# Laying the VectorE work of a gelu over three steps of a hand-written order instead of two

## The chip, the core and the metric

The kernel runs on one core of one Trainium2 chip. Its time is the device time of one execution in microseconds (us); the figure compared is the median of several runs. The engines are named as the profile names them: PE is TensorE's matmul, PEld its weight load, DVE is VectorE, ACT is ScalarE, POOL is GpSimd, SP is SyncE, whose queue issues most DMAs.

## The reference, cut to what matters

```python
x = A_x                                             # 1 x 2048 x 640
xn = layernorm(x)
qkv = xn @ wqkv                                     # 32 heads of 20
p = softmax(q @ k.T * 20 ** -0.5)                   # per head, 2048 x 2048
A = (p @ v) @ wo
y = layernorm(xn)
B = gelu(y @ w1 + b1) @ w2 + b2                     # 640 -> 1536 -> 640, tanh gelu
out = x + A + B
```

## The kernel before

**Stages.** A first stage normalises the tokens and forms q, k and v (to about 245 us of the span). The second stage is the attention of all heads, with the MLP's matmuls and all other small work woven into it by hand. A tail multiplies the attention's output by `wo` and adds everything up.

**The attention loop.** Heads go in pairs g = 0 to 15, queries in halves hf = 0 and 1 of 1024. The list `ORDER` runs pairs 0 to 11 with both halves, then half 0 of pairs 12 to 15, then half 1 of pairs 12 to 15. Each (g, hf) has eight groups: two blocks of 512 queries by four groups of four key blocks, 256 groups in all. One group writes four `scores` (two matmuls L600 each, into a PSUM buffer of three; ACT's exp L602 into a tile `p`), and for key blocks 0 and 1 of the four DVE forms the tile `low` (L614, in `rest`). At the group's end stands `pv` of the group before (L631), which needs that group's `p` and `low`.

**Two ticks a group.** Small work is written as Python generators, each `yield` of which ends a step. Twice a group (after the scores of key blocks 0 and 1, and after those of 2 and 3) the loop calls `tick()`, which takes one step of each generator in the list `sides`, then one of each in the list `patient`. A number behind `yield` is a cost in us of DVE work. It acts in one way: when the steps of `sides` in this tick, or of a generator begun since the last tick, have announced any cost, `patient` is passed over.

```python
t, taken[0] = taken[0], 0.0
for its in (sides, patient):
    if its is patient and t > 0:
        break
    for it in list(its):
        r = next(it, self_end)
        if r is self_end:
            its.remove(it)
        else:
            t += r or 0.0
```

The first tick of a group is followed by `low` of key block 0 and then by `other()`, which writes some matmuls of the MLP (`layer1` L823, `layer2` L855) or of the projection (L932); the second tick is followed by `low` of key block 1 and by `pv`. The 256 groups have ticks 1 to 512. After the last group, `more` writes three projection matmuls at a time (one step of the projection) and then a tick, so a tick there comes as often as three matmuls end.

**The gelu.** When the last matmul of a `layer1` pair has been written, `begin(gelu(...))` takes the gelu's first step on the spot and puts the rest in `sides`; 48 gelus are begun in all. Its first DVE operation, L758, reads the PSUM tile `pu`; that pool (`psM`) has one buffer, so PE's next MLP matmul waits for it. L759, L762 and L763 follow on DVE, ACT's tanh is L766, and L768 to L770 write `hT`.

**Finishing a block of heads.** When all pairs of a block are through (blocks end after pairs 3, 6, 9, 12, 14 and 16, for each half), `unload` appends a generator `finish` to `fins`, and if it is the only one there, starts `finishing()`, which takes the finishes one after another:

```python
if len(fins) == 1:
    (sides if hf == 1 and g + 1 >= TAIL else patient).append(finishing())
```

A finish loads the row sums (`lt`, L692) and the two partial outputs (`oa`, L714), inverts the sums on DVE (L719 to L726), stores them (`linv`, L728), loads them spread over rows (`rb`, L740), and for each half of 512 columns adds (L744), multiplies (L746), casts (L748), subtracts (L750) and stores `oscr` (L751). The `oa` and `rb` tiles have one buffer each. Between loads and first uses stand empty steps, four in most places. It ends with `ready[hf] += 1`. In the last finish, that of pairs 15 and 16 in half 1, `rb` comes from matmuls on PE (L735) and its DMAs go through ACT's queue; it waits 24 steps for `lt` and 17 for `rb`.

**The weights of `wo`.** `prep_late` runs in `sides` near the end of the attention. It splits `wo` on DVE (L560 to L572) in one step of cost 1.0 and then five times three steps of cost 0.6, 0.7 and 0.7: sixteen ticks in a row in which `patient` is passed over.

**The projection.** The output has eight pieces of 256 tokens, four of each half; each needs its part of `oscr` (`ot`, L887) and the MLP's sum (`acc`, L888), loaded by `load_piece`, and has four accumulations of 15 matmuls (L932), each ended by DVE's L893; L895 stores the result. Piece 0 is loaded by `ahead()` in `sides`, once `ready[0]` is 6 (all blocks of half 0). Pieces 4 to 7 need `ready[1]` at 6. After the attention the accumulations take PSUM buffers from the pool of the scores, of three.

Of the kernel before, what the change touches and what calls it, by code (L numbers as in the profile page):

```python
# [42 lines left out]
def mha_mlp_kernel(tc, x, wqkv, wo, w1, b1, w2, b2, out):  # L43
# [4 lines left out]
    with (  # L48
# [463 lines left out]
        with ExitStack() as scope:  # L512
# [241 lines left out]
            def gelu(ps, r2f, hT, f):  # L754
                u = m1.tile([P, 2, MC], F32, tag="u", name="u")
                w = m1.tile([P, 2, MC], F32, tag="w", name="w")
                scale_rows(r2f)
                nc.vector.tensor_mul(u, ps, r2f[:, None, :].to_broadcast([P, 2, MC]))  # L758
                nc.vector.tensor_add(u, u, b1t[:, f : f + 2, None].to_broadcast([P, 2, MC]))  # L759
                yield 1.2  # L760

                nc.vector.tensor_mul(w, u, u)  # L762
                nc.vector.scalar_tensor_tensor(w, w, 1.0 / 0.044715, u, ALU.add, ALU.mult)  # L763
                yield 1.2
                yield
                nc.scalar.activation(w, w, AF.Tanh, scale=0.7978845608028654 * 0.044715)  # L766
                yield
                nc.vector.scalar_tensor_tensor(u, w, 1.0, u, ALU.add, ALU.mult)  # L768
                nc.vector.tensor_scalar(hT[:, f : f + 2, 0, :], u, ch, None, ALU.mult)
                nc.vector.scalar_tensor_tensor(hT[:, f : f + 2, 1, :], u, ch, hT[:, f : f + 2, 0, :],  # L770
                                               ALU.mult, ALU.subtract)
                yield 1.7

            def scale_rows(r2f):

                if r2f in unscaled:
                    unscaled.remove(r2f)
                    nc.vector.tensor_scalar(r2f, r2f, f1, None, ALU.mult)
# [34 lines left out]
            def layer1(mc, f):  # L813
                xnt, r2f = xs[mc]
                if f == 0:
                    hTs[mc] = m0.tile([P, KF, 2, MC], F16, tag="hT", name="hT")
                ps = psM.tile([P, 2, MC], F32, tag="m", name="pu")
                for i in range(2):
                    n = 0
                    fo_ = (f + i) % 4 * P  # L820
                    for k in range(KD):
                        for a, b in PASS:
                            nc.tensor.matmul(ps[:, i], w1v[:, k, (f + i) // 4, a, fo_ : fo_ + P], xnt[:, k, b, :],  # L823
                                             start=(n == 0), stop=(n == 3 * KD - 1))
                            n += 1
                            if n % 3 == 0:
                                if i == 1 and n == 15:
                                    begin(gelu(ps, r2f, hTs[mc], f))
                                    over[0] = True
                                yield 0.3276  # L830
                if f == KF - 2:
                    if mc + 2 < NMC:
                        load_chunk(mc + 2)
                    if mc + 1 == NMC:
                        sides.append(ahead())
                        sides.append(prep_late("o", wot, wov, wo.rearrange("(k p) n -> p k n", p=P), KD,
                                               range(KD), 4))
# [291 lines left out]
```

## Time and profile before

| | |
|---|---|
| time, median of 3 runs | 1376.91 us (1376.67 to 1377.99) |
| profiled execution: time, span | 1378.13 us, 1376.4 us |
| PE, ACT, DVE busy in the span | 98%, 82%, 77% |
| ACT's exp L602, x1024 | 973.9 us busy, mean 1043 ns |
| DVE's `low` L614, x512 | 610.6 us busy, mean 1218 ns |
| DVE's L758, L759, L762, L763, x48 each | 684, 692, 692 and 692 ns mean |
| DVE's L768, L769, L770, x48 each | 685, 486 and 751 ns mean |
| ACT's tanh L766, x48 | 637 ns mean |

Busy times are unions over the span; a mean is that of one instruction. PE's matmuls overlap in the profile, so its 98% says that little of its time is seen as waiting, not that each matmul is at its fastest.

### The profile page before, as it was taken

The numbers are of one execution on the slowest core, as the hardware profiler recorded it, in microseconds if no ns is written. First come the engines' busy times: TensorE is split into PE (matmuls) and PEld (weight loads), VectorE is DVE, ScalarE is ACT, GpSimd is POOL, SyncE is SP. The second block draws the span as 40 slices with busy tenths as digits, with TensorE's granted clock in tenths as the row PEclk, the third lists the DMA queues.
The fourth block names the chain that finished last, engine by engine and source line by source line (L and its number), as shares of the span: only waits on it lengthen the run. The fifth ranks groups of instructions, "written<-read, shape, count | busy, mean of one in ns | idle before, by whom it ended". The sixth has DMA issues, their size and how long they took to land.

```text
span 1376.4 us, 29091 instructions
## 1 busy us (share of the span) xinstructions
PE 1347.3 (98%) x11711; PEld 599.3 (44%) x11711; DVE 1061.0 (77%) x1425; ACT 1125.5 (82%) x1282; POOL 32.6 (2%) x75
## 2 busy tenths in 40 slices
PE   8999998999999999999999999999999999999998
PEld 6555555443334333433343333343434434333375
DVE  6647753899778988788888778887978898898732
ACT  5644332999999999999999999999999999999700
POOL 2000000000000000000000000000000000000000
PEclk9999999999999999999999999999999999999999
DMA  9853413012113222213231123232123222244275
GB/s 266 226 187 115 99 58 114 3 33 62 52 38 100 81 76 68 70 47 82 67 99 40 47 66 89 64 83 62 41 57 113 73 76 77 65 135 119 89 235 177
DMA packets 92320, 125.68 MB, mean 91 GB/s; under 512 B 16905, under 2 KB 58569, under 8 KB 92178
## 3 DMA queue, kind: packets, MB, share of 16 engines
q1 hardware_dynamic: 89218, 117.14, 28.9%
q0 software_dynamic: 2304, 5.24, 2.2%
q8 instruction: 94, 1.54, 0.5%
q10 hardware_dynamic: 656, 1.36, 0.3%
q14 instruction: 48, 0.39, 0.1%
HBM read 80.84 MB, written 42.86 MB: 90 GB/s over the span
## 4 chain that ended last, share of the span: by engine, by line
PE 66%; DVE 8%; ACT 3%; DMA 2%; issue 2%; SPq 1%; DVEq 0%; ACTq 0%
PE o L631 26%; PE s L600 16%; PE py L855 11%; PE pu L823 9%; PE z L932 4%; DVE low L614 3%; ACT p L602 3%; DVE u L758 1%; DVE u L759 1%; DVE w L762 1%; DMA oscr<-oa 1%; DMA acc<-accscr 0%; DVE w L763 0%; DVE hT L770 0%; DVE u L768 0%
## 5 line engine op out<-in xcount | busy, mean ns | idle before, releaser
L602 ACT ACTIVATE p<-s 128x1024 f32<-128x1024 f32 x1024 | 973.9, 1043 | 46.2 <-PE s L600 38.9
L614 DVE TENSOR_TENSOR low<-p 128x1024 f16<-128x1024 f32 x512 | 610.6, 1218 | 162.4 <-ACT p L602 161.7
L631 PE MATMUL o<-p,vfull 128*32 128x512 bf16 (+1 forms) x4096 | 430.2, 493 | 0.0
L600 PE MATMUL s<-qs,ks 61*128 61x512 f16 x2048 | 317.3, 382 | 7.0 <-ACT p L602 5.5
L600 PEld LDWEIGHTS <-ks 61*128 61x128 f16 x2048 | 64.0, 94 | 294.4 <-issue 291.9
L823 PE MATMUL pu<-xm,w1t 128*128 128x256 f16 x1440 | 181.1, 275 | 3.8 <-DMA xm<-xscr 2.7
L855 PE MATMUL py<-w2t,hT 128*128 128x320 f16 x1152 | 178.6, 300 | 1.7 <-DVE u L758 1.1
L823 PEld LDWEIGHTS <-w1t 128*128 128x128 f16 x1440 | 131.5, 98 | 72.1 <-issue 57.8
L855 PEld LDWEIGHTS <-hT 128*128 128x128 f16 x1152 | 102.5, 98 | 89.3 <-issue 55.1
L286 PE MATMUL qkp<-xnt,wv 128*128 128x512 f16 x600 | 132.5, 379 | 0.2 <-DVE wv L383 0.2
L631 PEld LDWEIGHTS <-vfull 128*32 128x32 f16 x3072 | 60.4, 95 | 137.7 <-issue 106.3
L631 PE MATMUL o<-low,vfull 128*32 128x512 f16 x1024 | 103.5, 378 | 3.7 <-DVE low L614 3.7
L300 ACT ACTIVATE qkhl<-qkp,qks 128x1024 f16<-128x1024 f32 (+1 forms) x24 | 23.3, 971 | 82.9 <-PE qkp L286 65.4
L286 PEld LDWEIGHTS <-wv 128*128 128x128 f16 x600 | 58.1, 98 | 68.2 <-DVE wv L383 0.7
L631 PEld LDWEIGHTS o<-p,vfull 128*32 128x32 f32 x2048 | 62.1, 108 | 52.3
L932 PE MATMUL z<-w1t,ot 128*128 128x320 f16 x480 | 66.3, 299 | 1.4 <-DMA ot<-oscr 0.8
L349 PE MATMUL vp<-wv,xnt 128*128 128x320 f16 x480 | 66.6, 299 | 0.0
L932 PEld LDWEIGHTS <-ot 128*128 128x128 f16 x480 | 46.5, 98 | 21.9 <-issue 2.9
L349 PEld LDWEIGHTS <-xnt 128*128 128x128 f16 x480 | 46.5, 98 | 18.2
L893 DVE SCALAR_TENSOR_TENSOR acc<-z,sc,acc 128x320 f32<-128x320 f32 x32 | 17.5, 550 | 46.8 <-PE z L932 42.7
L301 DVE SCALAR_TENSOR_TENSOR qkhl<-qkp,qks,qkhl 128x1024 f16<-128x1024 f32 (+1 forms) x24 | 26.5, 1104 | 32.2 <-ACT qkhl L300 32.2
L652 ACT ACTIVATE ev<-o 128x512 f32<-128x512 f32 x64 | 39.5, 618 | 3.5 <-PE o L631 3.5
(168 smaller groups left out, 682.6 us busy)
## 6 DMA issues: line engine op xcount, KB each, us to landing
qkscr<-qkhl SPq DMA_DIRECT2D x40, 256.0 KB
opart<-ev SPq DMA_DIRECT2D x124, 80.0 KB
ks<-qkscr SPq DMA_DIRECT2D x120, 80.0 KB
qs<-qkscr SPq DMA_DIRECT2D x192, 40.0 KB
oa<-opart SPq DMA_DIRECT2D x32, 240.0 KB
xt<-in_A_x_dram SPq DMA_DIRECT2D x16, 320.0 KB
xscr<-xnt SPq DMA_DIRECT2D x4, 1280.0 KB
xm<-xscr SPq DMA_DIRECT2D x8, 640.0 KB
```

Of the source, the lines that this page charges most:

```text
L286: nc.tensor.matmul(ps[:, i, :], wv[:, k, q, a, mm * P : (mm + 1) * P], xnts[c][:, k, b, :], start=(k + n == 0), stop=(k == KD - 1 and n == 2))
L300: nc.scalar.activation(hl[:, 0, i0:i1], ps[:, i0:i1], AF.Copy, scale=a)
L301: nc.vector.scalar_tensor_tensor(hl[:, 1, i0:i1], ps[:, i0:i1], a, hl[:, 0, i0:i1], ALU.mult, ALU.subtract)
L349: nc.tensor.matmul(ps[:, hf, :320], xnts[c][:, k, a, j * P : (j + 1) * P], wv[:, k, 2, b, hf * 320 : (hf + 1) * 320], start=(n == 0), stop ...
L600: nc.tensor.matmul(ps[:, a, :], ks[64 * a : 64 * a + 61, kb * P : (kb + 1) * P], qs[64 * a : 64 * a + 61, cc * 512 : (cc + 1) * 512], star ...
L602: nc.scalar.activation(pt, ps, AF.Exp, scale=QS)
L614: nc.vector.tensor_sub(low, pt, upper(pt))
L631: nc.tensor.matmul(pv.o[32 * q : 32 * q + 32, :], src[:, v0 - PAD * (1 - q % 2) :][:, :32], t, start=q not in pv.begun, stop=last, skip_gr ...
L652: nc.scalar.activation(evs[g, hf][:, cc], pv.o, AF.Copy)
L823: nc.tensor.matmul(ps[:, i], w1v[:, k, (f + i) // 4, a, fo_ : fo_ + P], xnt[:, k, b, :], start=(n == 0), stop=(n == 3 * KD - 1))
L855: nc.tensor.matmul(ps[:, :320], hTs[mc][:, f, a, j * P : (j + 1) * P], w2v[:, f, b, hf * 320 : (hf + 1) * 320], start=(n == 0), stop=(n == ...
L932: nc.tensor.matmul(ps[:, :320], ot[:, k, a, j * P : (j + 1) * P], wov[:, k, b, h * 320 : (h + 1) * 320], start=(n == 0), stop=(n == 3 * KD ...
```

## The change

The gelu's first four DVE operations stood two and two in two steps, with an empty step behind them. They now stand one, two and one in three steps. The tanh and all that follows keep their steps. The costs announced to `tick()` go from 1.2, 1.2 and nothing to 0.6, 1.2 and 0.6. In the changed file L759 is line 760 and L763 is line 764.

```diff
                 nc.vector.tensor_mul(u, ps, r2f[:, None, :].to_broadcast([P, 2, MC]))
+                yield 0.6
                 nc.vector.tensor_add(u, u, b1t[:, f : f + 2, None].to_broadcast([P, 2, MC]))
+
+                nc.vector.tensor_mul(w, u, u)
                 yield 1.2
-
-                nc.vector.tensor_mul(w, u, u)
                 nc.vector.scalar_tensor_tensor(w, w, 1.0 / 0.044715, u, ALU.add, ALU.mult)
-                yield 1.2
-                yield
+                yield 0.6
                 nc.scalar.activation(w, w, AF.Tanh, scale=0.7978845608028654 * 0.044715)
```

## The prediction

> **What bounds the kernel now.** I read the windows first, then PE's waits in the attention, then two stretches in order of time.
>
> ```profile
> 250.00:1290.00 1040.00, 1027.07 (x9562) 410.94 (x9559) 883.21 (x1056) 998.55 (x1124) 13.98 (x16) 1.00 0.25 70
> 1303.00:1337.00 34.00, 33.26 (x260) 24.11 (x256) 13.33 (x24) 0.60 (x1) 0.00 (x0) 1.00 0.70 202
> ```
>
> The columns are length, busy PE, PEld, DVE, ACT, POOL, granted clock, DMA share, GB/s. In the attention PE is seen idle for 13 of 1040 us, ACT for 41; in the tail only PE and the transfers count.
>
> ```profile
> PE s L600 <- ACT p L602: 4.9, 17, 0.6
> PE o L631 <- DVE low L614: 3.7, 7, 0.8
> PE pu L823 <- DVE u L758: 1.1, 3, 0.5
> PE py L855 <- DVE u L758: 1.1, 2, 0.8
> PE py L855 <- DVE xb L787: 0.7, 1, 0.7
> ```
>
> These are PE's waits from 240 to 1290 us (total, times, longest). DVE causes 6.6 us. A typical stall in the timeline:
>
> ```profile
> 316.43 0.69 DVE L758 TENSOR_TENSOR u<-pu,r2f 128x512 f32<-128x512 f32 x1
> 317.15 0.69 DVE L759 TENSOR_TENSOR u<-u,b1t 128x512 f32<-128x512 f32 x1
> ...
> 317.88 0.69 DVE L762 TENSOR_TENSOR w<-u 128x512 f32<-128x512 f32 x1
> ...
> 318.60 0.69 DVE L763 SCALAR_TENSOR_TENSOR w<-w,u 128x512 f32<-128x512 f32 x1
> ...
> 319.21 2.35 DVE L614 TENSOR_TENSOR low<-p 128x1024 f16<-128x1024 f32 x2
> ...
> 320.48 0.40 PE L631 MATMUL o<-low,vfull 128*32 128x512 f16 x3 [0.53 <-DVE low L614]
> ```
>
> DVE runs four gelu operations, then the `low` that `pv` needs; PE waits 0.53 us. The end of the program, from the chain of waits:
>
> ```profile
> 1315.52 2.43 PE rb L735 x32
> ...
> 1324.27 1.22 DVE oa L744
> ...
> 1327.82 1.23 DVE oa L750
> 1329.06 0.02 issue
> 1329.08 3.16 DMA oscr<-oa
> ...
> 1332.73 4.24 DMA ot<-oscr
> ...
> 1337.02 25.98 PE z L932 x190
> ```
>
> The last finish is already the path: `rb` on PE, four DVE operations, the store, the load of piece 4, then PE, which has waited 0.76 us. So every us by which `rb` comes later is a us of the span.
>
> **The DVE order.** No operation is added. L758 and the two after it keep their places, for nothing stands between the first step and the next tick. Only L763 moves: behind the `low` of its group's second key block, ahead of the next group's first. That `low` comes 0.61 us earlier (L763's start to the next start, 318.60 to 319.21). All seven waits on `low` in the timeline (0.21, 0.76, 0.53, 0.53, 0.75, 0.49, 0.38) are waits for this `low`; 0.61 off each leaves 0.3, so 3.4 us go. The five waits on L758 (2.2) keep their cause, but ahead of four of them (0.52, 0.80, 0.29, 0.26) two or three operations of a finish stand in DVE's queue between two gelus, and with one step fewer for `patient` one of these (0.42 to 0.68) leaves: 0 to 1.8 us more. I take 1. PE turns a removed wait into time only where ACT follows it; ACT idles 38 us for PE, so mostly yes. Gain: 0 to 6.6, taken as **4 us**.
>
> The cover this needs: the tanh must not wait for L763. Its end lies 1.37 to 2.97 us ahead of the tanh's start over the 48 gelus (six under 1.8); it moves by one `low`, 1.14 us start to start. Cover remains, 0.2 us at the least; if it were gone, six stalls of ACT under 0.5 us, below 3 us in all.
>
> **The steps.** A gelu begun after tick b made `patient` be passed over in ticks b+1 (costs 1.2 and 1.2) and b+4 (1.7). Now b+2 announces 0.6, so it is three ticks, not two. Most finishes live in `patient` and come later, their DMAs on SP with them. In the attention each has slack: `ready` is needed by nobody before the projection. The end is different, and it can be counted out, since the order is fixed when the program is written. From tick 370 the patient list works without rest; ten gelus begin between 375 and 477.
>
> - Finish (16,0), pairs 15 and 16 in half 0: before, done in tick 482, just ahead of the `unload` of (14,1), which finds `fins` empty and so goes into `sides`. After, (16,0) is then at its first L744. So (14,1) queues behind it, in `patient`.
> - The sixteen costly ticks of `prep_late`, 491 to 506, pass (16,0) over between the L744 and L746 of its second half. Its last L750 and store are in tick 509, piece 0 is loaded in 510 and its matmuls begin behind tick 511. Before, that load was written in 483.
> - (14,1): before, ticks 483 to 504, two to a group. After, 511 to 531, and ticks after 512 last three matmuls, 0.41 us (12.33 us for 90).
> - (16,1): `rb` on PE behind tick 544 before, 560 after.
>
> **What that costs.** *First*, piece 0. In the trace DVE is free at 1292.3, at the place of the last L750 (0.68): end 1293.0. A store of this size took 2.03 us to release the next DMA (1269.76 to 1271.79), so the loads issue at 1295.0. For piece 4, first issue to first matmul was 4.73 us (1332.29 to 1337.02): 1299.8. PE wants piece 0 at 1295.83: it stands **4.0 us**, with the last `scores` and `pv` behind it. Bounds: 3 if DVE is free sooner, 6 if the loads queue. Its `acc`, 7.2 from issue to use at piece 4 (1333.36 to 1340.60), comes at about 1303.7, just ahead of its L893.
>
> *Second*, (14,1) inside the tail. Its four-step gaps were 8 us of attention and are 1.6 us now, so DVE meets its loads unfinished, and L893, which frees PE's buffers, is queued behind. With PE 4.0 late: piece 0's first L893 follows its first matmul by 4.5 (1295.83 to 1300.36) and takes 0.55, the inversion of `lt` 1.3 (1313.58 to 1314.85): 1306.2; `linv` out and back to `rb`'s issue 2.48 (1250.53 to 1253.01), four issues 1.4, landing 2.1: L746 at 1311.9; L750 ends 1314.3; its store must land before `oa` may be loaded again, 1316.4; that load (3.4 in the chain) 1320; four operations of 2.5: 1322.5. The L893 of piece 1's first accumulation stands behind: PE, three buffers ahead, waits 1319.1 to 1323.1. Then the load of piece 2, queued on SP behind the second store, issues at 1323 and lands 4.7 later: PE starts piece 2 at 1327.7, where it would have been at 1320.8 (the 4.0 in). That is **6.9 us**; bounds 0 (transfers in time) and 12 (each of the six slower by 0.9).
>
> *Third*, `rb` is 16 steps later in PE's own order: 48 matmuls of 0.137 = **6.6 us**, with little spread.
>
> Piece 4 follows `rb` by the same chain as before (21.5 us, 1315.52 to 1337.02), so the sum is 4.0 + 6.9 + 6.6 = 17.5 us; after piece 4 all is as before. Minus 4: +13.5. From the profiled execution, 1378.13, that is 1391.6; it ran 1.2 above the median of 1376.91, so I predict **1390.4**.
>
> The fit in the Trainium skill, "DMA: Bandwidth & Descriptors", section "Anatomy of one DMA — SWDGE (gpsimd) path", is 2.0 us and bytes over 436 GB/s. By it the 0.16 MB store takes 2.4 us and the 0.66 MB pair of loads 3.5, an estimate that would make the first term 3.2 us instead of 4.0; the trace's 2.03 and 4.73 stand in the sum, since the loads run beside others.
>
> **Rivals.**
> - *The waits of (14,1) are absorbed* (second term 0): +10.6 - 4 = +6.6, 1383.5. For it: DVE waits 42.7 us for PE in the tail, so has room. Against: three buffers are 6 us, and two round trips through DRAM stand in a row. 0.15.
> - *ACT bounds the attention, so nothing is gained there*: +17.5, 1394.4. For it: 998.55 of 1040 us busy. Against: it idles for PE, hardly ever the reverse. 0.09. The Trainium skill's "Perfetto Trace Analysis", section "Identifying the Most-Contended Engine", judges ACT by its busy share and says matmul busy is no measure for PE; by that rule ACT is the bound and this is the outcome.
> - *Transfers crowd in the tail*: output stores, pieces and `rb` share SP's queue at 202 GB/s; each round trip a third longer, +9: 1399. 0.08.
> - *Faster*: the late finishes hide behind pieces 0 to 3, and the gain alone is left: -5, 1372. It decides if `rb` can be 6.6 us later without piece 4 waiting. Against: PE waited 0.76 us there already. 0.05.
> - *Nothing moves* (stalls return elsewhere, tail hidden): 1377. 0.03.
>
> **The numbers.** The forecast has 0.60, with its own range of 1385 to 1396. With the first two rivals and the edge of the third the range is 1381 to 1399. A difference below 0.2%, 2.8 us, could not be told from none: faster 0.05, same 0.05 (with the low end of the first rival), slower 0.90.
>
> **What would show it.** Right: waits of PE on `low` under 1 us in all; PE waiting 3 to 6 us for `ot` near 1296, several us for L893 or `ot` near piece 1 and 2, about 7 us before piece 4; the attention's last `pv` group reached 4 us sooner. Wrong: `rb` on PE before 1325 us, piece 4 without a wait, or new waits in the attention.

## The result and the profile after

| | before | changed |
|---|---|---|
| median | 1376.91 us (5 runs) | 1392.37 us (1391.58 to 1393.09, 5 runs) |
| profiled execution: time, span | 1378.13, 1376.4 us | 1393.09, 1391.3 us |

The ratio on record is 1.0101, 95% interval 1.0086 to 1.0117; the two medians above give 1.0112, inside it. (All ratios below are those on record, and differ a little from those of the medians.) The change costs about 15 us. The span divides cleanly: the attention became shorter and the tail became much longer. PE's waits from 240 to 1290 us, in the changed kernel (total, times, longest):

```profile
PE s L600 <- ACT p L602: 5.2, 18, 0.6
PE py L855 <- DVE u L758: 0.9, 2, 0.5
PE pu L823 <- DVE u L758: 0.3, 1, 0.3
```

The seven waits on `low` are gone, those on L758 are down from 2.2 to 1.2, and the one on L787 (0.7) is gone too. How much time this gave is read from ACT's copy L652, which stands once at the end of each block of 512 queries. Its first and its last but one are shown, from the timeline of the kernel before and then of the changed one:

```profile
257.75 0.60 ACT L652 ACTIVATE ev<-o 128x512 f32<-128x512 f32 x1
...
1287.59 0.60 ACT L652 ACTIVATE ev<-o 128x512 f32<-128x512 f32 x1 [0.24 <-PE o L631]
```

```profile
258.36 0.60 ACT L652 ACTIVATE ev<-o 128x512 f32<-128x512 f32 x1
...
1281.39 0.63 ACT L652 ACTIVATE ev<-o 128x512 f32<-128x512 f32 x1
```

The changed kernel reaches its first L652 0.61 us later and its last but one 6.20 us earlier: **the attention gained 6.8 us**. (When the first L652 comes differs by up to 3.5 us between the traces of this document, one for each kernel, though the kernels differ by no more than one gelu ahead of it; so gains are read between two L652, and the tail from the last but one to the end of the span.) The whole span is still 14.9 us longer, so **the tail lost 21.1 us**. The chain of waits in the changed tail:

```profile
1297.81 2.87 DMA linv<-lt
...
1301.80 3.26 DMA rb<-linv
1305.14 0.69 DVE oa L746
...
1307.37 3.35 DMA oscr<-oa
...
1311.14 4.73 DMA oa<-opart
1316.06 0.70 DVE oa L744
...
1320.23 7.03 DMA acc<-accscr
1327.38 0.55 DVE acc L893
...
1329.25 2.47 PE rb L735 x32
...
1346.12 4.29 DMA ot<-oscr
1350.46 27.29 PE z L932 x190
```

What was PE alone before (1303 to 1315) is now a row of round trips through DRAM: out with `linv`, back with `rb`, out with `oscr`, back with `oa`. `rb` on PE starts at 1329.25 instead of 1315.52, though PE reached the tail 6 us sooner. PE's own rows say what it waited for:

```profile
1290.69 0.45 PE L932 MATMUL z<-w1t,ot 128*128 128x320 f16 x2 [1.02 <-DMA ot<-oscr]
1291.79 1.53 PE L932 MATMUL z<-w1t,ot 128*128 128x320 f16 x10 [0.66 <-DMA ot<-oscr]
...
1319.16 4.07 PE L932 MATMUL z<-w1t,ot 128*128 128x320 f16 x17 [8.37 <-DVE acc L893]
1323.97 4.79 PE L932 MATMUL z<-w1t,ot 128*128 128x320 f16 x34 [0.74 <-DMA ot<-oscr]
...
1349.08 0.71 PE L932 MATMUL z<-w1t,ot 128*128 128x320 f16 x2 [5.84 <-DMA ot<-oscr]
```

Piece 0, the end of piece 1, piece 2 and piece 4: the four places of the prediction. A fifth, not foreseen, is small: ahead of `rb` PE waited 0.49 us for L726, the inversion of `lt`, which stood on DVE behind an L893 that waited 3.83 us for `acc`.

### The profile page after: what moved, and what is told of

It reads as the page before. It is cut to its first block, busy times and chain, and to the rows that moved or that the text cites. A ratio compares the mean times of both kernels' runs of the same rounds, so it can differ in the third digit from the quotient of the medians.

```text
span 1391.3 us, 29084 instructions
## 1 busy us (share of the span) xinstructions
PE 1349.0 (97%) x11711; PEld 600.1 (43%) x11711; DVE 1058.3 (76%) x1425; ACT 1124.4 (81%) x1282; POOL 32.4 (2%) x75
## 4 chain that ended last, share of the span: by engine, by line
PE 67%; DVE 7%; ACT 4%; DMA 2%; issue 2%; SPq 0%; DVEq 0%; ACTq 0%
PE o L631 26%; PE s L600 17%; PE py L855 11%; PE pu L823 9%; ACT p L602 3%; PE z L932 3%; DVE low L614 3%; DMA ot<-oscr 1%; DVE u L758 1%; DMA acc<-accscr 1%; DVE hT L770 0%; DMA oscr<-oa 0%; DVE u L768 0%; DVE u L760 0%; DVE w L762 0%
## 5 line engine op out<-in xcount | busy, mean ns | idle before, releaser
L932 PE MATMUL z<-w1t,ot 128*128 128x320 f16 x480 | 70.2, 308 | 17.9 <-DVE acc L893 9.0
L893 DVE SCALAR_TENSOR_TENSOR acc<-z,sc,acc 128x320 f32<-128x320 f32 x32 | 17.3, 545 | 50.6 <-PE z L932 46.6
L652 ACT ACTIVATE ev<-o 128x512 f32<-128x512 f32 x64 | 39.7, 620 | 3.3 <-PE o L631 3.3
```

Of the source, the lines that this page charges most:

```text
L652: nc.scalar.activation(evs[g, hf][:, cc], pv.o, AF.Copy)
L932: nc.tensor.matmul(ps[:, :320], ot[:, k, a, j * P : (j + 1) * P], wov[:, k, b, h * 320 : (h + 1) * 320], start=(n == 0), stop=(n == 3 * KD ...
```

## The experiments

The theory: the moved operation is a gain, and all the loss comes from the finishes, which are passed over once more per gelu and so fall into the tail. The rival: laying the operations over three steps is itself worse.

**Order without cost.** The changed kernel, the third step announcing nothing.

```diff
                 nc.vector.scalar_tensor_tensor(w, w, 1.0 / 0.044715, u, ALU.add, ALU.mult)
-                yield 0.6
+                yield
```

> The changed kernel, its third step announcing no cost (0.6 to nothing). The VectorE order of the gelu stays changed, the finishes get their old ticks back: (16,0) done in tick 482, rb behind tick 544. Theory (the loss is all in the late finishes, the moved L763 is a gain): the attention's gain of 6.2 us stays, the tail is as before, 1370.7 us (1369 to 1373). Rival (three steps are themselves worse, or the gain came from the finishes being spread): the gain shrinks, 1375 to 1378, or the loss stays, 1390.

Measured: 1370.91 us (1370.49 to 1371.61, 7 runs) against 1378.03 for the kernel before beside it, ratio 0.9938, 0.9916 to 0.9959. The same places in its chain:

```profile
1308.40 2.43 PE rb L735 x32
...
1329.80 25.98 PE z L932 x190
```

Both are 7.1 to 7.2 us ahead of the kernel before, as is the end of the span: the tail is the old one. From the first to the last but one L652 it gained 5.6 us, a little less than the 6.2 expected; the other 1.5 lie ahead of the first L652 (256.26 instead of 257.75) and are not put down to the change. The theory holds and the rival falls. This version beats both kernels.

**Cost without order.** The kernel before, its empty step announcing 0.6.

```diff
                 yield 1.2
-                yield
+                yield 0.6
                 nc.scalar.activation(w, w, AF.Tanh, scale=0.7978845608028654 * 0.044715)
```

> The kernel before, its empty step announcing 0.6. No VectorE operation of a gelu moves; the finishes come as late as in the changed kernel (rb behind tick 560). Theory: the tail loses the 21 us of the changed kernel, the attention gains little (0 to 2, from finishes no longer standing two between gelus): 1396 to 1398 us. Rival (the loss needs the moved operations): 1376 to 1380.

Measured: 1396.7 us (1394.79 to 1399.21), ratio 1.0134, 1.0098 to 1.0171. PE's waits on `low` are those of the kernel before, 3.7 us in seven; between the two L652 it gained 1.4 us. Its tail lost 21.0 us, as much as the changed kernel's. One number behind a `yield`, with no instruction of the gelu moved, costs the tail. The two gains add up: 5.6 + 1.4 against 6.8 in the changed kernel.

**The ticks of prep_late.** The changed kernel with all costs of `prep_late` taken out.

```diff
-                yield 1.0
+                yield
...
-                    yield 0.6
+                    yield
...
-                        yield 0.7
+                        yield
```

> The changed kernel, prep_late announcing no costs. Finish (16,0) is then done in tick 493 instead of 509, (14,1), still in the patient list, in 517, rb behind 546. Theory (the sixteen ticks passed over are what turns a slip of 11 ticks into the loss): attention gain kept, two steps of 0.4 us lost in the tail and some DVE crowding, 1371 to 1375 us. Rival (that (14,1) lands in the patient list is enough by itself): 1384 or more.

Measured: 1373.61 us (1371.77 to 1375.59, 11 runs), ratio 0.9968, 0.9955 to 0.9982. The attention kept its 6.8 us, and the tail lost 2.0 instead of 21.1. So a slip of 11 ticks, with (14,1) standing in the patient list, costs a tenth of the loss (the median is 2.7 us above the first experiment's). It is the sixteen ticks passed over that turn the slip into 21 us.

**The costs of the gelu.** The first experiment's kernel, all three early steps announcing nothing.

```diff
-                yield 0.6
+                yield
                 nc.vector.tensor_add(u, u, b1t[:, f : f + 2, None].to_broadcast([P, 2, MC]))

                 nc.vector.tensor_mul(w, u, u)
-                yield 1.2
+                yield
```

> The first experiment's kernel with the gelu's three early steps announcing nothing at all, so the finishes are served in nearly every tick and are done earlier (16,0 in tick 476). Theory (the costs of the gelu matter only for when finishes end): as the first experiment, 1371 us, within 1. Rival (the costs keep finish operations out of the gelu's bunch, and that is worth something): 1372.5 to 1376, with PE's waits on L758 or low back at several us.

Measured: 1374.45 us (1372.97 to 1374.99, 11 runs). That is 3.5 us slower than the first experiment and in the rival's range. Between the two L652 it gained 3.7 us instead of 5.6, though the waits shown grew by 0.7 us only (0.4 on `low` instead of none, 1.9 on L758 instead of 1.6), not by several. DVE and then PE near 855 us, from the timeline:

```profile
853.82 0.69 DVE L762 TENSOR_TENSOR w<-u 128x512 f32<-128x512 f32 x1
854.43 0.68 DVE L746 TENSOR_TENSOR oa<-oa,rb 120x512 f32<-120x512 f32 x1
855.03 1.22 DVE L614 TENSOR_TENSOR low<-p 128x1024 f16<-128x1024 f32 x1
```

```profile
856.30 0.40 PE L631 MATMUL o<-low,vfull 128*32 128x512 f16 x3 [0.36 <-DVE low L614]
```

With no cost announced a finish's L746 takes the place that L763 left, ahead of the same `low`, and PE waits again. So the costs of the first two steps are worth 1.9 us of attention. Both fall into the same tick, which the second's 1.2 alone would close to `patient`; the two were not run apart. The third's cost is not worth its number.

**A longer gap in the tail.** The changed kernel with 24 empty steps ahead of the second half of finish (14,1), and 4 instead of 24 in the last finish so that `rb` keeps its place.

```diff
-            W1, W2 = 24, 17
+            W1, W2 = 4, 17
...
-                    for _ in range(W2 if last else 4):
+                    for _ in range(W2 if last else 24 if (g1, hf, c0) == (14, 1, 512) else 4):
```

> The changed kernel with 24 empty steps instead of 4 ahead of the second half of finish (14,1), and 4 instead of 24 ahead of the row sums of the last finish, so that rb stays behind tick 560. VectorE then meets the oa reload after it has landed, and piece 2 is loaded before the second store is queued. Theory (the second term is VectorE standing in its queue for that reload, ahead of L893): PE's waits of 8.4 and 0.7 us before piece 2 go, 1383 us (1381 to 1386). Rival (transfers in the tail are short of bandwidth whatever their order): 1389 or more.

Measured: 1389.41 us (1387.48 to 1389.77): 3.0 us gained, not 9, which is the rival's range. The wait on L893 at the end of piece 1 is gone, as the theory said, but another has come, for piece 2. PE's row and SP's queue:

```profile
1317.66 0.72 PE L932 MATMUL z<-w1t,ot 128*128 128x320 f16 x2 [5.06 <-DMA ot<-oscr]
```

```profile
1306.43 0.34 SPq L751 DMA_DIRECT2D oscr<-oa  x1
1310.22 0.78 SPq L714 DMA_DIRECT2D oa<-opart  x2
...
1313.83 1.83 SPq L887 DMA_DIRECT2D ot<-oscr  x2
```

The reload of `oa` (L714) is issued 3.8 us behind the store that it waits for, and the load of piece 2 (L887) stands behind it in the same queue. Whether the queue or slow transfers hold piece 2, this run does not tell; the next one does.

**Those DMAs in a queue of their own.** The same kernel with the DMAs of finish (14,1) issued by GpSimd.

```diff
-                go = dma(g1 - 1, hf)
+                go = nc.gpsimd.dma_start if (g1, hf) == (14, 1) else dma(g1 - 1, hf)
```

> The kernel of the gap experiment (1389.41 us), with the DMAs of finish (14,1) issued by GpSimd instead of SP, so that piece 2 is no longer loaded behind them in SP's queue. Theory (two queues in a row make the second term: VectorE's, ahead of L893, and SP's, ahead of piece 2's load): PE's wait of 5.1 + 0.5 us for piece 2 goes, rb starts 5.6 us earlier, 1383.8 us (1382 to 1386). Rival (the transfers themselves are late): the wait stays above 3 us, 1387 us or more.

Measured: 1395.11 us (1393.98 to 1395.66). The wait for piece 2 fell from 5.06 and 0.51 to 0.99 and 0.62, so SP's queue was what held it, and the rival, that this wait stays above 3 us, falls. The time is nevertheless longer, not shorter, since GpSimd's queue made a wait of its own:

```profile
1327.08 4.50 PE L735 MATMUL rb<-lt,sel 64*80 64x64 f32 x32 [6.44 <-DVE lt L726]
```

The second `oscr` store was issued there at 1324.26 and the copies `sel` that `rb` multiplies by came behind it, to 1326.3; DVE, held by the same late reload, began the inversion of `lt` 0.6 us later than in the gap experiment and ended L726 at 1326.9; beside those copies its L725 took 1.52 us instead of 0.19, for a reason that no run shows. So `rb` started 1.75 us later than in the gap experiment, and after the long wait PE ran at half clock: `rb` took 4.50 us instead of 2.43, the 54 matmuls behind it 9.28 instead of 7.46. Whether the wait for piece 2 can be removed without a new one, and the expected 1383.8 reached, is not shown.

**rb earlier in the order.** The changed kernel with 8 instead of 24 empty steps in the last finish.

```diff
-            W1, W2 = 24, 17
+            W1, W2 = 8, 17
```

> The changed kernel with 8 instead of 24 empty steps ahead of the row sums of the last finish, which puts rb back behind tick 544. Theory (the third term is the order alone): 48 matmuls of 0.137, 6.6 us less, 1385.8 us (1384.5 to 1388), piece 4 waiting at most 1 us. Rival (the last finish then stands behind finish (14,1) on VectorE or behind its own transfers): under 3 us less, 1389.5 to 1392.

Measured: 1386.37 us (1385.17 to 1386.95), 6.0 below the changed kernel, in the theory's range. The spans differ by 6.6, but 1.7 of that lie ahead of the first L652 (256.64 and 258.36); the tail gained 4.8. PE had 108 matmuls of the projection ahead of `rb` again instead of 156, so the order is what moved it. That the gain is the full 6.6 of these 48 matmuls is not shown: PE ran at half clock in more places here (last section).

**The cost until late.** The changed kernel, the third step announcing 0.6 only until six finishes are done.

```diff
-                yield 0.6
+                yield 0.6 if sum(ready) < 6 else None
```

> The changed kernel, its third step announcing 0.6 until six finishes are done (tick 340 on) and nothing after. The finishes keep out of the gelus' way for most of the attention and still end as before (16,0 in tick 482). Theory (the two gains of the attention add, 5.6 from the moved operation and 1.2 to 1.4 from the spaced finishes, and the tail is as before): 1.2 us below the first experiment, 1369.7 us (1368.5 to 1371), and from the first to the last but one ev of the trace 6.5 to 7 us gained on before. Rival (the spacing is worth nothing where the ends agree): 1371 us, 5.6 gained.

Measured: 1371.89 us (1369.64 to 1374.40, 6 runs), not below the first experiment: the rival's case. Between the two L652 it gained 6.0 us, 0.3 above that one and not 1.2. In the changed kernel 1.1 us of the gain come between the last two of the L652 compared (16.16 us apart instead of 17.27), where PE waited for L787 in the kernel before (0.66 us, at 1279): the operations of (14,1) are no longer there. So most of what looked like a gain from spacing is the other side of the late finish.

## Why the prediction was right, point by point

The likeliest case came: 1390.4 forecast, 1392.37 measured, in the case's own range. That the attention gains and the tail loses more, and why, is settled by the first two experiments. The sizes, from the profiled executions:

| step | forecast | measured | from |
|---|---|---|---|
| attention | -4 | -6.8 | L652, first to last but one |
| first: piece 0 | +4.0 | +2.0 | its first matmuls end at 1293.33; PE, due there at 1289.60, would have ended them at 1291.34 |
| second: (14,1) in the tail | +6.9 | +11.4 | from PE's due time at piece 0 to `rb`: 39.65 us, before 19.62; less the 2.0 above and the 6.6 below |
| third: order of `rb` | +6.6 | +6.6 | 156 instead of 108 matmuls ahead of `rb`: 48 of 0.137 |
| after piece 4's start | 0 | +1.5 | 1350.46 to 1391.3, against 1337.02 to 1376.4 |

With the 0.6 of the first stage and 0.3 less between `rb` and piece 4 (21.2 us, 21.5 before), the sum is 15.0 of 14.9.

**How much of it is luck.** The mechanism was right: the order counted in ticks, the four places, and a gain ahead of a larger loss. The total is nearer than its terms by luck: the errors of -2.8, -2.0, +4.5 and +1.5 nearly cancel. Of the signs that were to show it, PE's wait for `ot` near 1296 was to be 3 to 6 us and was 1.68, and the last `pv` was to come 4 us sooner and came 6.2; the others came. Two sums of the forecast are a little off. In the second term L746 should stand at 1312.2 instead of 1311.9, and piece 2's place without the wait at 1321.1 instead of 1320.8, which leaves the 6.9 as it is. The rival *Faster* has a gain of 5 where the forecast has 4.

**The attention term was too small.** Which stalls would go was right: all seven on `low`, half of the time on L758, and the tanh never had to wait. But each was priced by the idle time that the profile shows, as far as 0.61 us of it. In the first experiment the waits shown fell by 4.3 us (3.65 on `low`, 0.6 on L758), and L652 moved by 5.6; the first three stalls, shown as 0.21, 0.76 and 0.53, moved the following L652 by 0.61, 0.68 and 0.69. So the idle shown does not give the size of a stall here. PE's ends are modelled in the profile, which may be the reason; no run shows it. Another 1.1 us of the 6.8 are not the moved operation at all, but (14,1) leaving the end of the attention (last experiment).

**The first term was too large**, at "A store of this size took 2.03 us to release the next DMA". The two rows of SP, changed kernel:

```profile
1286.30 0.34 SPq L751 DMA_DIRECT2D oscr<-oa  x1
1286.68 1.07 SPq L887 DMA_DIRECT2D ot<-oscr  x2
```

The load did not wait for the store's landing: piece 0 has the first 256 queries, and the store writes columns 512 to 1023. The forecast's 2.03 was for a reload into the stored tile, which is another wait. The load took 5.1 us to PE's first uninterrupted matmul (1286.68 to 1291.79), against 4.73 taken.

**The second term was too small**, by round trips that the forecast took from quieter places. From `linv`'s issue to the freeing of PE's buffers (L893 at 1318.57) the forecast had 16.3 us and the trace has 20.8: `linv` out 2.9 against 2.48, store and release of `oa` 3.4 against 2.03, its reload 5.3 (1310.78 to 1316.06) against 3.6, `rb` from first issue to use 4.45 against 3.2. PE's wait for L893 became 8.37 instead of 4.0, and piece 2's 0.74 instead of 2.6, since its load ran meanwhile. Two things that the forecast had at nothing are in the 11.4 as well: after the 8.37 the next 17 matmuls took 1.7 us more than at full clock, and PE waited 0.49 us ahead of `rb`. By the fit of the Trainium skill, "DMA: Bandwidth & Descriptors", section "Anatomy of one DMA — SWDGE (gpsimd) path", the estimates would have been 2.4 for the store and 3.5 for the pair of loads of the first term; on SP's queue in this tail the trace has 3.4 and 5.1.

**The rivals.** Absorbed waits: ruled out by the 8.37. ACT as the bound: ruled out, since the attention gained. Crowded transfers: the round trips were 4.5 us longer than taken, half of the 9 priced; that crowding made them so is not shown. *Faster*: ruled out, piece 4 waited 5.84 us. *Nothing moves*: ruled out by the 15 us.

## What to carry to other kernels

In an order written by hand, a cost that only steers who is served next is a change of everything that is served by it: count each deferred queue through to its last customer before trusting that it has slack. A consumer that just makes a rendezvous (here finish (16,0), done in the tick in which the next one looked) has no slack at all, and gaps sized for long steps fail when the work falls into a stretch of short ones. Moving one operation behind the one PE waits for was most of the attention's gain (5.6 of 6.8 us); it came without a loss in the tail once the served order was left alone.

## What the runs showed that was not expected

**Waits of PE cost clock as well.** After PE's wait of 8.37 us the next 17 matmuls took 4.07 us, where 0.137 each would be 2.3. The windows of the changed kernel around it (the last column but two is the granted clock):

```profile
1314.00:1319.00 5.00, 0.00 (x0) 0.00 (x0) 2.83 (x5) 0.00 (x0) 0.00 (x0) 0.66 0.39 114
1319.00:1323.90 4.90, 4.07 (x17) 2.21 (x16) 1.58 (x4) 0.00 (x0) 0.00 (x0) 0.65 0.75 189
```

It happened again after the wait for piece 4 (clock 0.50 from 1350 to 1352), where 190 matmuls took 27.29 us instead of 25.98: 1.3 of the 1.5 us in the last row of the table. In the early-`rb` kernel `rb` took 4.49 us instead of 2.43 after a wait of 7.1. The Trainium skill, "TensorE: Matmul & The Clock Gate", section "Part 1: The HAM clock gate", has half rate after an idle window of about 3.4 us and full rate after as much sustained work; for these long waits the trace agrees (clock 0.50 from 1319 to 1322, 0.77 in the next microsecond), and the prediction had left it out of its stalls.

Short waits close together did it too. In the cost-only kernel PE waited 0.79 and 1.05 us for piece 0:

```profile
1290.60:1294.06 3.46, 1.62 (x12) 0.43 (x9) 2.61 (x3) 2.74 (x3) 0.00 (x0) 1.00 0.93 260
1294.06:1297.50 3.44, 3.44 (x18) 1.30 (x20) 0.76 (x1) 0.37 (x1) 0.00 (x0) 0.50 1.08 341
```

Its ten matmuls of piece 0 took 2.66 us, those of the early-`rb` kernel (waits of 0.89 and 0.93) 2.76 and those of the own-queue kernel (0.79 and 1.30) 2.85. In the changed kernel, with 1.02 and 0.66, they took 1.53 at full clock. Which busy share decides, the runs do not show; single waits under 1 us in the attention left the clock at 1.00.
